# Moving table passes of a setup to the scalar engine, and starting a fold between two tables

## The chip, the core and the metric

The kernel runs on one core of a Trainium2 chip. The profile shows five engines: TensorE (PE; its weight loads are PEld), VectorE (DVE), ScalarE (ACT), GpSimd (POOL) and the sync engine (SP). They run side by side (in the first 24 us of the kernel before, TensorE, VectorE, ScalarE and GpSimd are busy for 10.5, 20.4, 20.6 and 18.7 us), and it shows what each waits for. Here GpSimd starts the loads. The metric is the device time of one execution in microseconds (us). The kernel before is steady: 49 runs of it in this study lie between 609.36 and 610.03 us, mean 609.66.

## The reference

```python
X = np.fft.fft(np.fft.fft(x, axis=1), axis=2).real     # x: 8 x 3008 x 256
h = np.maximum(X.transpose(0, 2, 1) @ w_tok1, 0) @ w_tok2
u = X + h.transpose(0, 2, 1)
out = u + np.maximum(u @ w_ch1, 0) @ w_ch2
```

The Fourier transforms are done as matrix products, so the kernel first makes tables of cosines and sines on the chip. This setup, the first 24 us of 608, is all that the change touches.

## The kernel before

The setup has four strands that meet in the first real product `pw`:

- the angles `vp`, `vq`, reduced to one period on VectorE and ScalarE, and their sines `tp`, `tq` on ScalarE;
- two turned copies `tt` of each table: TensorE transposes, ScalarE evicts (copies the finished accumulator away, so that it is free again), TensorE multiplies by an anti-identity (`pr`, a matrix with ones on the other diagonal), ScalarE evicts again;
- the cosine table of the first product, `td0` and `td1`, out of the angles `md`;
- batch 0: rows `xp` and, by two gathers (loads by an index list), `xm` are loaded, the fold adds and subtracts mirrored halves on VectorE (12 pieces, giving `eo`), `front` multiplies them (`pz`) and evicts to `z`.

```python
def reduced(v, r, m, period):                 # on VectorE; TWO23 is 2**23, added to round
    ts(v, m, 1.0 / period, AT.mult, TWO23, AT.add)
    ts(v, v, -TWO23, AT.add, -float(period), AT.mult)
    nc.vector.tensor_tensor(out=r, in0=v, in1=m, op=AT.add)

def filler(n):                                # products whose result nobody reads
    pw = ps_out("filler")
    for _ in range(n):
        nc.tensor.matmul(pw[:, 0:P], lhsT=ident[:], rhs=ident[:], start=True, stop=True)

# front(b): six blocks of five products, three accumulators in rotation
for t0 in (11, 6, 1):
    for half in range(2):
        pz = ps_f("pz")
        for k in range(5):
            nc.tensor.matmul(pz[:, 96*k:96*k+96], lhsT=eo[:, t0+k, c], rhs=..., ...)
        copy(b == 0 and half and t0 < 11, zo[...], pz[...])   # true: VectorE, false: ScalarE
        yield
# two small pz blocks (yield after each), then the pw products ...

# ... cut: index columns, loads, identity tables, angles ...
ts(md[:, 0:128], jrow[:, 1:129], pcol[:], AT.mult, 64.0, AT.add)
ts(md[:, 128:255], jrow[:, 1:128], pcol[:], AT.mult)
reduced(vd[:], md[:], md[:], 256)
# ... cut ...
table_d()                                     # the two sines td, then small corrections on GpSimd
turn(tp, tts_p, 8)                            # transposes, then 8 fillers
turn_rows(tts_p, 1.0, 0)
take(fold(0, [nc.vector] * 4), 12)
own = front(0)
take(own, 2)
turn(tq, tts_q, 4)
take(own, 4)
turn_rows(tts_q, -1.0, 0)
take(own, 2)
filler(8)
take(own, 2)                                  # the first pw products
```

Of the kernel before, what the change touches and what calls it, by code (L numbers as in the profile page):

```python
# [9 lines left out]
FP16 = mybir.dt.float16  # L10
FP32 = mybir.dt.float32
I32 = mybir.dt.int32
AT = mybir.AluOpType
AFT = mybir.ActivationFunctionType
# [5 lines left out]
P = 128  # L20
BB = 8
S = 3008
D = 256
DTOK = 256
# [5 lines left out]
NG = 12  # L30
# [5 lines left out]
TWO23 = float(2.0 ** 23)  # L36
# [4 lines left out]
def kernel(  # L41
# [9 lines left out]
    nc = tc.nc  # L51
# [8 lines left out]
    const = ctx.enter_context(tc.tile_pool(name="const", bufs=1))  # L60
# [5 lines left out]
    def ps_mm(name):  # L66
        return psum.tile([P, 512], FP32, tag="mm", name=name, bufs=3)
# [7 lines left out]
    def dram(t, offset, ap):  # L75
        return bass.AP(tensor=t, offset=offset, ap=ap)

    def iota(t, pattern, base, cm):
        nc.gpsimd.iota(t, pattern=pattern, base=base, channel_multiplier=cm,
                       allow_small_or_imprecise_dtypes=True)  # L80

    def pvec(name, dt=FP32):
        return const.tile([P, 1], dt, tag=name, name=name)

    def ts(out_, in_, s1, op0, s2=None, op1=None, eng=nc.vector):
        if op1 is None:
            eng.tensor_scalar(out=out_, in0=in_, scalar1=s1, scalar2=None, op0=op0)
        else:
            eng.tensor_scalar(out=out_, in0=in_, scalar1=s1, scalar2=s2,
                              op0=op0, op1=op1)  # L90



    pcol, xicol, qcol = (pvec(n) for n in ("pcol", "xicol", "qcol"))
    iota(pcol[:], [[0, 1]], 0, 1)
    ts(xicol[:], pcol[:], float(NQ), AT.is_ge)
    nc.vector.scalar_tensor_tensor(out=qcol[:], in0=xicol[:], scalar=-float(NQ),
                                   in1=pcol[:], op0=AT.mult, op1=AT.add)
# [5 lines left out]
    jrow = const.tile([P, 129], FP32, tag="jrow")  # L104
# [3 lines left out]
                                   op0=AT.mult, op1=AT.add)  # L108
    ts(rowi[:], rowi[:], -2.0, AT.mult)
    ts(ix8[:], ix8f[:], rowi[:], AT.add, 0.0, AT.max)  # L110

    x8 = dram(x_t, 0, [[8 * D, BB * S // 8], [1, 8 * D]])

# [20 lines left out]
    def gdma(out_, in_):  # L134
        nc.gpsimd.dma_start(out=out_, in_=in_)


    setup = ctx.enter_context(ExitStack())
    stage = setup.enter_context(tc.tile_pool(name="stage", bufs=1))
    gen = setup.enter_context(tc.tile_pool(name="gen", bufs=1))  # L140
    w1p = stage.tile([P, NG, DTOK], FP16, tag="w1p")
    w1m = stage.tile([P, NG, DTOK], FP16, tag="w1m")
    tp, tq = (const.tile([P, NG, P], FP16, tag=n, name=n) for n in ("tp", "tq"))
    nc.scalar.activation(out=pvec("sin0")[:], in_=pcol[:], func=AFT.Sin, scale=0.0)
    for t in (tp, tq):
        for i in range(2):
            h = slice(64 * i, 64 * i + 64)
            nc.scalar.activation(
                out=t[h, :, 64 - 64 * i:128 - 64 * i],
                in_=pcol[h, :].unsqueeze(2).to_broadcast([64, NG, 64]),  # L150
                func=AFT.Copy, scale=0.0)
    nc.scalar.activation(out=w1m[64:128, NG - 1, :],
                         in_=pcol[64:128, :].to_broadcast([64, DTOK]),
                         func=AFT.Copy, scale=0.0)

    x_tiles = {0: load_x(0)}

# [7 lines left out]
                                   op0=AT.mult, op1=AT.add)  # L165
# [6 lines left out]
                                   op0=AT.mult, op1=AT.add)  # L172
    nc.vector.scalar_tensor_tensor(out=reff[:], in0=eq32[:], scalar=1472.0, in1=reff[:],
                                   op0=AT.mult, op1=AT.add)
# [3 lines left out]
                                   op0=AT.mult, op1=AT.add)  # L178
    nc.vector.scalar_tensor_tensor(out=offq[:], in0=mid[:], scalar=-752.0, in1=tmp[:],
                                   op0=AT.mult, op1=AT.add)  # L180
# [40 lines left out]
    def reduced(v, r, m, period):  # L221
# [4 lines that stand above are left out]
    def sin(out_, in_, period):  # L226
        nc.scalar.activation(out=out_, in_=in_, func=AFT.Sin, scale=PI2 / period)

    def table3(tab, r):
        for i in range(2):  # L230
            h = slice(64 * i, 64 * i + 64)
            sin(tab[h, :, h], r[h, :, :], S)
# [12 lines left out]
            copy(0, tts[0][:, 768 * h:768 * h + 768], pt[:, 0:768])  # L245
        filler(warm)

    def turn_rows(tts, sgn, warm):
        for h in range(3):
            pr = ps_mm("pr")  # L250
            nc.tensor.matmul(pr[:], lhsT=anti[:], rhs=tts[0][:, 512 * h:512 * h + 512],
                             start=True, stop=True)
            nc.scalar.activation(out=tts[1][:, 512 * h:512 * h + 512], in_=pr[:],
                                 func=AFT.Copy, scale=sgn)
        filler(warm)


    def filler(n):
        pw = ps_out("filler")
        for _ in range(n):  # L260
            nc.tensor.matmul(pw[:, 0:P], lhsT=ident[:], rhs=ident[:], start=True,
                             stop=True)

    def copy(e, out_, in_):
        if e:
            (nc.vector, nc.gpsimd)[e - 1].tensor_copy(out=out_, in_=in_)
        else:
# [9 lines left out]
    gp = gen.tile([P, NG], FP32, tag="gp")  # L277
    mp, vp, mq, vq = (gen.tile([P, NG, 64], FP32, tag=n, name=n)
                      for n in ("mp", "vp", "mq", "vq"))
    up, down = pvec("up"), pvec("down")  # L280
    nc.vector.memset(up[:], TWO23)
    nc.vector.memset(down[:], -TWO23)
    ts(gp[:], jrow[:, 0:NG], r2[:], AT.mult, offp[:], AT.add)
    nc.vector.scalar_tensor_tensor(
        out=mp[:], in0=jrow[:, 0:64].unsqueeze(1).to_broadcast([P, NG, 64]),
        scalar=r47[:], in1=gp[:].unsqueeze(2).to_broadcast([P, NG, 64]),
        op0=AT.mult, op1=AT.add)
# [5 lines left out]
    for o, i, scale, bias in ((mq, mp, 1.0, dq), (vq, mq, 1.0 / S, up),  # L293
                              (vq, vq, 1.0, down)):
        nc.scalar.activation(out=o[:], in_=i[:], func=AFT.Identity, scale=scale,
                             bias=bias[:])

    ident = const.tile([P, P], FP16, tag="ident")
    ts(ident[:], jrow[:, 0:P], pcol[:], AT.is_equal)
    anti = const.tile([P, P], FP16, tag="anti")  # L300
    acol = pvec("acol")
    ts(acol[:], pcol[:], -1.0, AT.mult, 127.0, AT.add)
    ts(anti[:], jrow[:, 0:P], acol[:], AT.is_equal)

    mask0, q24 = pvec("mask0"), pvec("q24")
    ts(mask0[:], xicol[:], -1.0, AT.mult, 1.0, AT.add)
    ts(q24[:], qcol[:], 24.0, AT.add)
# [3 lines left out]
    for a, n, col, off in ((0, 2, qcol, 47 / 4), (2, 2, qcol, 0.0), (4, 1, q24, 47 / 8)):  # L311
# [4 lines left out]
    sin(cs[:], m1[:], 47)  # L316
    reduced(vp[:], vp[:], mp[:], S)
    table3(tp, vp)
    nc.vector.scalar_tensor_tensor(out=vq[:], in0=vq[:], scalar=-float(S), in1=mq[:],
                                   op0=AT.mult, op1=AT.add)  # L320
    table3(tq, vq)
    for i, m in ((0, mask0), (1, xicol)):
        ts(t1n[:, :, i, :], cs[:, i:4:2, :], m[0:KR, :], AT.mult)
    ts(t1b[:, 1, :], cs[:, 4, :], float(np.sqrt(0.5)), AT.mult,
       xicol[0:KR, :], AT.mult)
    nc.vector.tensor_copy(out=t1b[:, 0:3:2, :], in_=t1n[:, :, 0, :])

    md, vd = (gen.tile([P, 255], FP32, tag=n, name=n) for n in ("md", "vd"))
    ts(md[:, 0:128], jrow[:, 1:129], pcol[:], AT.mult, 64.0, AT.add)
    ts(md[:, 128:255], jrow[:, 1:128], pcol[:], AT.mult)  # L330
    reduced(vd[:], md[:], md[:], 256)
    td0 = const.tile([P, 131], FP16, tag="td0")
    td1 = const.tile([P, P], FP16, tag="td1")
    alt = const.tile([P, 131], FP16, tag="alt")
# [3 lines left out]
    tcol, sgn = pvec("tcol"), pvec("sgn")  # L338
# [5 lines left out]
    ts(perm[:], jrow[:, 0:P], tcol[:], AT.is_equal, sgn[:], AT.mult, eng=pl)  # L344

    def table_d():
        sin(td0[:, 2:130], md[:, 0:128], 256)
        sin(td1[:, 1:P], md[:, 128:255], 256)
        pl.memset(td0[:, 0:1], 1.0)
        ts(td0[:, 1:2], td0[:, 129:130], 0.5, AT.mult, 0.5, AT.add, eng=pl)  # L350
        ts(td0[:, 130:131], td0[:, 129:130], 0.5, AT.mult, -0.5, AT.add, eng=pl)
        ts(td0[0:1, :], td0[0:1, :], 0.5, AT.mult, eng=pl)

        pl.memset(td1[:, 0:1], 0.0)
        pl.memset(td1[0:1, 0:1], 0.5)
        pl.memset(alt[:], 1.0)
        pl.memset(alt[:, 2:129:2], -1.0)
        pl.memset(alt[:, 130:131], 0.0)
# [33 lines left out]
    def fold(b, engs):  # L392
        xp, xm = x_tiles.pop(b)
        eo = perb.tile([KR, NR, D], FP16, tag="eo", name="eo")
        state[b] = {"eo": eo}
        add, sub = AT.add, AT.subtract
        for s, (t0, t1) in enumerate(((13, 17), (9, 13), (5, 9), (1, 5))):
            tt = engs[s].tensor_tensor
            t = slice(t0, t1)
            rv = slice(16 - t0, 16 - t1 if t1 < 17 else None, -1)  # L400
            if s == 0:
                tt(out=xp[:, 1:NR, 0], in0=xp[:, 1:NR, 0], in1=xm[0:KR, ::-1, 0], op=add)
                tt(out=eo[:, :, 0], in0=xp[:, :, 0], in1=xp[:, :, 0], op=add)
            tt(out=xp[:, t, 1:D], in0=xp[:, t, 1:D], in1=xm[0:KR, rv, D - 1:0:-1], op=add)
            yield
            if t0 == 1:
                t = slice(0, t1)
            tt(out=eo[:, t, 1:129], in0=xp[:, t, 1:129], in1=xp[:, t, 255:127:-1], op=add)
            yield
            tt(out=eo[:, t, 129:256], in0=xp[:, t, 1:128], in1=xp[:, t, 255:128:-1],  # L410
               op=sub)
            yield
# [304 lines left out]
    def take(g, n):  # L717
        for _ in range(n):
            next(g, None)

    table_d()
    turn(tp, tts_p, 8)
    turn_rows(tts_p, 1.0, 0)
    take(fold(0, [nc.vector] * 4), 12)
    own = front(0)
    take(own, 2)
    turn(tq, tts_q, 4)
# [31 lines left out]
    for b in range(BB):  # L759
        nxt = front(b + 1) if b + 1 < BB else iter(())  # L760
        folds = fold(b + 2, [nc.vector] * 4) if b + 2 < BB else None
        for c in range(NCH):
# [6 lines left out]
            for s in range(4):  # L769
                sub = 4 * c + s  # L770
                n = plan[b > 0][sub]
# [76 lines left out]
```

## Time and profile before

| | kernel before |
|---|---|
| time, median of the first 3 runs | 609.57 us (609.36 to 609.90) |
| first TensorE instruction | 12.36 us |
| first `pw` product | 23.32 us |
| first product into `pt`, from where TensorE works almost without a pause | 30.4 us |

Three lines of the profile's page: busy time by engine, the granted clock of TensorE in 40 slices (9 is 0.9 or more), and the engines' shares in the chain that ended last.

```profile
PE 586.7 (97%) x6278; PEld 420.1 (69%) x6278; DVE 455.8 (75%) x1021; ACT 441.2 (73%) x992; POOL 147.4 (24%) x233
...
PEclk9999999999999999999999999999999999999999
...
PE 91%; DVE 6%; ACT 2%; issue 0%; DVEq 0%; POOL 0%; POOLq 0%
```

TensorE bounds all but the setup. What the setup loses before the first `pw` shifts everything after it. The chain of waits shows who holds it up (start, duration, engine, tile, line):

```profile
9.62 0.97 DVE vp L224
...
10.61 0.84 ACT tp L227
...
14.05 0.51 ACT td L227 x2
14.56 1.40 ACT tt L268 x2
...
17.71 0.97 ACT z L268 x2
18.69 1.39 ACT tt L268 x2
20.07 0.72 ACT z L268
...
20.84 0.47 PE pz L424 x5
...
22.24 1.03 DVE z L266 x2
...
23.32 0.23 PE pw L451
```

VectorE is the chain up to 10.6 us, then ScalarE to 20.8 us. The last ScalarE `z` frees the third accumulator, and the last five `pz` products wait for it. The instructions in order of time, with the idle time before them in brackets, show room on both engines:

```profile
10.61 1.69 ACT L227 ACTIVATE tp<-vp 64x768 f16<-64x768 f32 x2 [1.71 <-DVE vp L224]
...
11.92 0.27 DVE L89 TENSOR_SCALAR md<-jrow,pcol 128x128 f32<-128x128 f32 x1
...
13.33 0.43 DVE L224 TENSOR_TENSOR md<-vd,md 128x255 f32<-128x255 f32 x1
13.68 0.21 DVE L402 TENSOR_TENSOR xp<-xp,xm 94x16 f16<-94x16 f16 x1
```

ScalarE idles 1.71 us before `tp`. VectorE spends 11.92 to 13.7 us on the angles `md`, and only then begins the fold.

### The profile page before, as it was taken

Reading aid. Unit: us, or ns where it says so; the run is one execution under the profiler, and the core shown is the slowest. Engines: PE = TensorE matmul, PEld = TensorE weight load, DVE = VectorE, ACT = ScalarE, POOL = GpSimd, SP = SyncE. Lnnn points to the kernel's source line nnn. Section 1 sums busy time; section 2 is a strip of 40 time slices with the busy share of each in tenths; the row PEclk is TensorE's granted clock in tenths of the full one; section 3 lists DMA queues with packets and bytes.
Section 4 is the critical chain, followed back from the end, with each engine's and each line's share of the span. In section 5 each row is a group of like instructions: output and inputs, shape, how many; then the busy total and the mean of one; then the engine's idle time right before and its main releaser. Section 6 shows DMA issues by size and latency. Waiting matters only on the chain.

```text
span 607.9 us, 15617 instructions
## 1 busy us (share of the span) xinstructions
PE 586.7 (97%) x6278; PEld 420.1 (69%) x6278; DVE 455.8 (75%) x1021; ACT 441.2 (73%) x992; POOL 147.4 (24%) x233
## 2 busy tenths in 40 slices
PE   1999999999999999999999999999999999999996
PEld 1756767667777677766777667766687667766675
DVE  8869689658887598757988689756979666665672
ACT  8876886777777777686777777677776877767772
POOL 8400414111242112401314222411131112111131
PEclk9999999999999999999999999999999999999999
DMA  9994924733249535673429233493341423234524
GB/s 150 210 190 104 179 57 82 134 69 78 54 91 158 70 53 86 107 117 53 91 51 176 62 76 75 77 178 53 53 74 47 92 54 83 58 70 60 90 58 100
DMA packets 86601, 56.53 MB, mean 93 GB/s; under 512 B 54864, under 2 KB 83472, under 8 KB 85776
## 3 DMA queue, kind: packets, MB, share of 16 engines
q1 hardware_dynamic: 78048, 37.84, 34.0%
q0 software_dynamic: 8256, 17.49, 16.6%
q8 instruction: 49, 0.80, 0.5%
q14 instruction: 24, 0.20, 0.1%
q10 hardware_dynamic: 224, 0.20, 0.1%
HBM read 34.98 MB, written 24.64 MB: 98 GB/s over the span
## 4 chain that ended last, share of the span: by engine, by line
PE 91%; DVE 6%; ACT 2%; issue 0%; DVEq 0%; POOL 0%; POOLq 0%
PE pc L583 39%; PE px L624 23%; PE py L624 9%; PE pu L543 7%; PE po L681 4%; PE pt L473 3%; PE pz L424 2%; DVE w L454 1%; PE py L501 1%; PE pq L501 1%; PE pw L451 1%; PE pw L452 1%; DVE sb L600 1%; ACT tt L268 0%; DVE osb L609 0%
## 5 line engine op out<-in xcount | busy, mean ns | idle before, releaser
L586 ACT ACTIVATE c<-pc 128x512 f16<-128x512 f32 (+1 forms) x572 | 295.9, 595 | 38.8 <-PE pc L583 20.8
L609 POOL TENSOR_TENSOR osb<-osb,rt 128x256 f32<-128x256 f32 x84 | 81.2, 967 | 377.5 <-DVE osb L609 367.7
L583 PE MATMUL pc<-ut,wc1p 128*128 128x512 f16 x576 | 140.5, 379 | 0.0
L624 PEld LDWEIGHTS <-c 128*128 128x128 f16 x2016 | 121.4, 98 | 20.7 <-issue 1.3
L583 PE MATMUL pc<-ut,wc1m 128*128 128x512 f16 (+1 forms) x576 | 134.9, 370 | 0.0
L551 DVE TENSOR_TENSOR ut<-pu,yt 128x512 f16<-128x512 f32 (+1 forms) x96 | 64.6, 674 | 53.3 <-PE pu L543 53.1
L624 PEld LDWEIGHTS <-sb 128*128 128x128 f16 x1512 | 89.9, 98 | 10.8 <-DVE sb L600 0.7
L629 ACT ACTIVATE m<-px 128x256 f32<-128x256 f32 x126 | 48.5, 385 | 66.9 <-PE px L624 41.5
L583 PEld LDWEIGHTS <-wc1p 128*128 128x128 f16 x576 | 52.1, 98 | 49.2 <-issue 2.6
L583 PEld LDWEIGHTS <-wc1m 128*128 128x128 f16 x576 | 53.0, 98 | 46.4
L624 PE MATMUL px<-wst,c 128*128 128x128 f16 x1008 | 70.8, 219 | 0.2 <-DVE c L600 0.2
L624 PE MATMUL px<-wc,c 128*128 128x128 f16 x1008 | 63.1, 219 | 0.0
L268 ACT ACTIVATE z<-pz 128x480 f16<-128x480 f32 (+1 forms) x60 | 40.2, 673 | 16.9 <-PE pz L424 11.0
L600 DVE TENSOR_TENSOR sb<-sb,c 128x768 f16<-128x768 f16 x84 | 50.2, 598 | 2.9
L609 DVE TENSOR_TENSOR osb<-py,m 128x256 f32<-128x256 f32 x84 | 35.1, 418 | 22.2 <-ACT m L629 17.4
L600 DVE TENSOR_TENSOR sb<-c 128x768 f16<-128x768 f16 x84 | 49.3, 587 | 2.4 <-ACT c L586 2.4
L543 PE MATMUL pu<-w2p,uu 128*128 128x512 f16 (+1 forms) x168 | 50.0, 379 | 0.0
L454 DVE SCALAR_TENSOR_TENSOR w<-alt,pw 128x131 f16<-128x131 f16 x96 | 33.0, 350 | 21.1 <-ACT w L268 20.5
L600 DVE TENSOR_TENSOR sb<-c,sb 128x768 f16<-128x768 f16 x84 | 47.1, 561 | 0.0
L600 DVE TENSOR_TENSOR c<-c 128x768 f16<-128x768 f16 x84 | 46.5, 554 | 0.0
L508 DVE TENSOR_TENSOR yt<-py,qs 128x512 f16<-128x512 f32 x48 | 30.9, 685 | 15.2 <-ACT qs L504 15.0
L624 PE MATMUL py<-wst,sb 128*128 128x128 f16 x504 | 35.2, 219 | 0.5 <-DVE sb L600 0.5
(163 smaller groups left out, 678.4 us busy)
## 6 DMA issues: line engine op xcount, KB each, us to landing
out_dram<-osb SPq DMA_DIRECT2D x83, 256.0 KB, 3.7
xp<-in_x_dram POOLq DMA_DIRECT2D x16, 272.0 KB
out_dram<-osb SPq DMA_DIRECT2D x11, 192.0 KB, 3.2
xp<-in_x_dram POOLq DMA_DIRECT2D x16, 127.5 KB
rt<-ut SPq DMA_TRANSPOSE x96, 3.8
w2s<-in_moe_w_tok_dram POOLq DMA_DIRECT2D x1, 1504.0 KB
w1p<-in_moe_w_tok_dram POOLq DMA_DIRECT2D x2, 384.0 KB
wc<-in_moe_w_ch_dram POOLq DMA_DIRECT2D x1, 768.0 KB
```

What stands on the lines that cost most here:

```text
L268: nc.scalar.activation(out=out_, in_=in_, func=AFT.Copy)
L454: nc.vector.scalar_tensor_tensor(out=w[:, g, 0:131], in0=alt[:], scalar=pw[:, 131:132], in1=pw[:, 0:131], op0=AT.mult, op1=AT.add)
L508: nc.vector.tensor_tensor(out=yt[:, h, CW * c:CW * c + CW], in0=py[:], in1=qs[:], op=op)
L543: nc.tensor.matmul(pu[:, 0:n], lhsT=uu[:, th, int(minus), h, :], rhs=w2_cols(b, c)[:, th], start=(th == 0), stop=(th == 1))
L551: nc.vector.tensor_tensor(out=ut[:, h, 0:n].rearrange("p (a b) -> p a b", b=64), in0=pu[:, 0:n].rearrange("p (b a) -> p a b", b=64), in1=y ...
L583: nc.tensor.matmul(pc[:, 0:n], lhsT=wc[:, h, ct * P:(ct + 1) * P], rhs=ut[:, h, 0:n], start=(h == 0), stop=(h == 1))
L586: nc.scalar.activation(out=c1[:, ct, 0:n], in_=pc[:, 0:n], func=AFT.Relu)
L600: nc.vector.tensor_tensor(out=o, in0=x, in1=y, op=op)
L609: eng.tensor_tensor(out=o, in0=x, in1=y, op=AT.add)
L624: nc.tensor.matmul(o[:, t], lhsT=a(k)[:, f:f + P], rhs=w(k), start=(first and t == 0 and k == 0), stop=(k == HC - 1), skip_group_check=True)
L629: nc.scalar.activation(out=m[:, i], in_=pa[:, 0], func=AFT.Copy)
L681: nc.tensor.matmul(po[0:n, o:o + D], lhsT=c1[:, ct, ks * P:ks * P + n], rhs=wc2[:, ct, :], start=(ct == 0), stop=(ct == NCT - 1))
```

## The change

Its intent is to give ScalarE's idle time work that VectorE does, and to start the fold earlier. The passes over `md` and `vd` go to ScalarE, ahead of its zero fills, which stay on it. The identity tables come after `vp` on VectorE. The last pass over `md` and the two `td` sines come after six of the twelve fold pieces. The argument `on_vector` of `turn_rows`, which the change also adds, is never used.

```diff
+    nc.scalar.activation(out=md[:, 0:128], in_=jrow[:, 1:129], func=AFT.Identity,
+                         scale=pcol[:], bias=quarter[:])
+    nc.scalar.activation(out=md[:, 128:255], in_=jrow[:, 1:128], func=AFT.Copy,
+                         scale=pcol[:])
+    for i, scale, bias in ((md, 1.0 / 256, up), (vd, 1.0, down)):
+        nc.scalar.activation(out=vd[:], in_=i[:], func=AFT.Identity, scale=scale,
+                             bias=bias[:])
     # ... the zero fills of tp, tq, w1m, moved up with these ...
-    ident / anti built before the angle reductions
     reduced(vp[:], vp[:], mp[:], S)
     table3(tp, vp)
+    ident / anti built here; the pass over vq after the t1n tables
-    ts(md[:, 0:128], jrow[:, 1:129], pcol[:], AT.mult, 64.0, AT.add)
-    ts(md[:, 128:255], jrow[:, 1:128], pcol[:], AT.mult)
-    reduced(vd[:], md[:], md[:], 256)
     def table_d():
+        nc.vector.scalar_tensor_tensor(out=md[:], in0=vd[:], scalar=-256.0, in1=md[:],
+                                       op0=AT.mult, op1=AT.add)
         sin(td0[:, 2:130], md[:, 0:128], 256)
-    table_d()
     turn(tp, tts_p, 8)
     turn_rows(tts_p, 1.0, 0)
-    take(fold(0, [nc.vector] * 4), 12)
+    pieces = fold(0, [nc.vector] * 4)
+    take(pieces, 6)
+    table_d()
+    take(pieces, 6)
```

(The two lines on the identity tables stand for moved blocks. The constants `up`, `down` and `quarter` are filled earlier too, which is cut here.)

More of the change, by code (lines that the diff above doesn't have):

```diff
@@ L90, in ts @@
                               op0=op0, op1=op1)
+    setup = ctx.enter_context(ExitStack())
+    stage = setup.enter_context(tc.tile_pool(name="stage", bufs=1))
+    gen = setup.enter_context(tc.tile_pool(name="gen", bufs=1))
+    w1p = stage.tile([P, NG, DTOK], FP16, tag="w1p")
+    w1m = stage.tile([P, NG, DTOK], FP16, tag="w1m")
+    tp, tq = (const.tile([P, NG, P], FP16, tag=n, name=n) for n in ("tp", "tq"))
+    up, down, quarter = (pvec(n) for n in ("up", "down", "quarter"))
+    nc.vector.memset(up[:], TWO23)
+    nc.vector.memset(down[:], -TWO23)
+    nc.vector.memset(quarter[:], 64.0)
     pcol, xicol, qcol = (pvec(n) for n in ("pcol", "xicol", "qcol"))
@@ L110 @@
     ts(ix8[:], ix8f[:], rowi[:], AT.add, 0.0, AT.max)
+    nc.scalar.activation(out=pvec("sin0")[:], in_=pcol[:], func=AFT.Sin, scale=0.0)
+    md, vd = (gen.tile([P, 255], FP32, tag=n, name=n) for n in ("md", "vd"))
+    nc.scalar.activation(out=md[:, 0:128], in_=jrow[:, 1:129], func=AFT.Identity,
[5 more added lines that the diff above has]
+                             bias=bias[:])
+    for t in (tp, tq):
+        for i in range(2):
+            h = slice(64 * i, 64 * i + 64)
+            nc.scalar.activation(
+                out=t[h, :, 64 - 64 * i:128 - 64 * i],
+                in_=pcol[h, :].unsqueeze(2).to_broadcast([64, NG, 64]),
+                func=AFT.Copy, scale=0.0)
+    nc.scalar.activation(out=w1m[64:128, NG - 1, :],
+                         in_=pcol[64:128, :].to_broadcast([64, DTOK]),
+                         func=AFT.Copy, scale=0.0)
     x8 = dram(x_t, 0, [[8 * D, BB * S // 8], [1, 8 * D]])
@@ L135, in gdma @@
         nc.gpsimd.dma_start(out=out_, in_=in_)
-    setup = ctx.enter_context(ExitStack())
-    stage = setup.enter_context(tc.tile_pool(name="stage", bufs=1))
-    gen = setup.enter_context(tc.tile_pool(name="gen", bufs=1))
-    w1p = stage.tile([P, NG, DTOK], FP16, tag="w1p")
-    w1m = stage.tile([P, NG, DTOK], FP16, tag="w1m")
-    tp, tq = (const.tile([P, NG, P], FP16, tag=n, name=n) for n in ("tp", "tq"))
-    nc.scalar.activation(out=pvec("sin0")[:], in_=pcol[:], func=AFT.Sin, scale=0.0)
-    for t in (tp, tq):
-        for i in range(2):
-            h = slice(64 * i, 64 * i + 64)
-            nc.scalar.activation(
-                out=t[h, :, 64 - 64 * i:128 - 64 * i],
-                in_=pcol[h, :].unsqueeze(2).to_broadcast([64, NG, 64]),
-                func=AFT.Copy, scale=0.0)
-    nc.scalar.activation(out=w1m[64:128, NG - 1, :],
-                         in_=pcol[64:128, :].to_broadcast([64, DTOK]),
-                         func=AFT.Copy, scale=0.0)
     x_tiles = {0: load_x(0)}
@@ L246, in turn, with turn_rows @@
         filler(warm)
-    def turn_rows(tts, sgn, warm):
+    def turn_rows(tts, sgn, warm, on_vector=()):
         for h in range(3):
@@ L252, in turn_rows @@
                              start=True, stop=True)
-            nc.scalar.activation(out=tts[1][:, 512 * h:512 * h + 512], in_=pr[:],
-                                 func=AFT.Copy, scale=sgn)
+            o = tts[1][:, 512 * h:512 * h + 512]
+            if h in on_vector:
+                ts(o, pr[:], sgn, AT.mult)
+            else:
+                nc.scalar.activation(out=o, in_=pr[:], func=AFT.Copy, scale=sgn)
         filler(warm)
@@ L279 @@
                       for n in ("mp", "vp", "mq", "vq"))
-    up, down = pvec("up"), pvec("down")
-    nc.vector.memset(up[:], TWO23)
-    nc.vector.memset(down[:], -TWO23)
     ts(gp[:], jrow[:, 0:NG], r2[:], AT.mult, offp[:], AT.add)
@@ L296 @@
                              bias=bias[:])
-    ident = const.tile([P, P], FP16, tag="ident")
-    ts(ident[:], jrow[:, 0:P], pcol[:], AT.is_equal)
-    anti = const.tile([P, P], FP16, tag="anti")
-    acol = pvec("acol")
-    ts(acol[:], pcol[:], -1.0, AT.mult, 127.0, AT.add)
-    ts(anti[:], jrow[:, 0:P], acol[:], AT.is_equal)
     mask0, q24 = pvec("mask0"), pvec("q24")
@@ L318 @@
     table3(tp, vp)
-    nc.vector.scalar_tensor_tensor(out=vq[:], in0=vq[:], scalar=-float(S), in1=mq[:],
-                                   op0=AT.mult, op1=AT.add)
-    table3(tq, vq)
+    ident = const.tile([P, P], FP16, tag="ident")
+    ts(ident[:], jrow[:, 0:P], pcol[:], AT.is_equal)
+    anti = const.tile([P, P], FP16, tag="anti")
+    acol = pvec("acol")
+    ts(acol[:], pcol[:], -1.0, AT.mult, 127.0, AT.add)
+    ts(anti[:], jrow[:, 0:P], acol[:], AT.is_equal)
     for i, m in ((0, mask0), (1, xicol)):
@@ L326 @@
     nc.vector.tensor_copy(out=t1b[:, 0:3:2, :], in_=t1n[:, :, 0, :])
-    md, vd = (gen.tile([P, 255], FP32, tag=n, name=n) for n in ("md", "vd"))
-    ts(md[:, 0:128], jrow[:, 1:129], pcol[:], AT.mult, 64.0, AT.add)
-    ts(md[:, 128:255], jrow[:, 1:128], pcol[:], AT.mult)
-    reduced(vd[:], md[:], md[:], 256)
+    nc.vector.scalar_tensor_tensor(out=vq[:], in0=vq[:], scalar=-float(S), in1=mq[:],
+                                   op0=AT.mult, op1=AT.add)
+    table3(tq, vq)
     td0 = const.tile([P, 131], FP16, tag="td0")
@@ L346, in table_d @@
     def table_d():
+        nc.vector.scalar_tensor_tensor(out=md[:], in0=vd[:], scalar=-256.0, in1=md[:],
+                                       op0=AT.mult, op1=AT.add)
         sin(td0[:, 2:130], md[:, 0:128], 256)
```

## The prediction

> **What bounds the kernel now.** The page shows TensorE busy 97% of the 607.9 us span at 0.9 or more of its clock in every slice; the chain that ended last is 91% PE. Only the first stretch is not PE's: it begins at 12.36 us and is fed properly only from about 23.3 us. Busy time by stretches gives for 0 to 24 us: PE 10.5, DVE 20.4, ACT 20.6. The change touches only this stretch (the instruction order is otherwise the same), so the stake is a shift of everything after 24 us, a few us at most.
>
> **The chain of waits** is DVE up to 10.6 us (identity tables 0.58 us, `vp` ready at 10.58). From 10.61 to 20.79 it is almost wholly ACT, without a gap: sines of `tp`, `tq` (3.4 us), two `td` sines (0.5), `tt` copies (1.4), `tt` from `pr` (1.8), `z` (1.1), `tt` (1.4), `z`. ACT sat idle 1.71 us before `tp`, for DVE `vp`.
>
> **What the change moves.**
> 1. DVE loses five passes over `md`/`vd` (11.92 to 13.7 us in the timeline, about 1.75 us) and gains one combined pass (this form took 0.95 at 768 elements; estimate for 255: 0.4), after six fold pieces.
> 2. ACT gains four passes. 768 elements with one pointer operand took 0.94[...]. Zero fills, `mq`, `vq`, `cs` move later by this; `cs` ends at 10.2 to 10.6 instead of 8.9.
> 3. The identity tables leave the path to `vp`: ready near 9.95 instead of 10.58.
>
> ACT's idle 1.71 us is thus eaten by its new passes: `tp` begins at 10.1 to 10.55 instead of 10.61. `tq` waits for DVE `vq`, now after the identities and `t1n`: 12.0 to 12.2 (was 12.33).
>
> 4. The fold could begin on DVE near 12.1 instead of 13.68, but its data are not there: the landing times in the trace put the end of the second `xm` gather at 13.0 us. The fold starts near 13.05 after almost 1 us of idle, six pieces end near 16.5 (17.1 before), the `md` pass near 16.9.
> 5. The `td` sines leave the place before `tt` but stand before the first `z`; ACT must still do both before `z`. `tt` starts 0.6 to 0.8 us earlier, `z` only 0.1 to 0.3 us (17.3 to 17.5, was 17.60).
>
> From there ACT's order is unchanged. So of about 1.35 us net taken from DVE only 0.1 to 0.3 us reaches the first `pw` product (23.32 before), and the rest shifts with it. GpSimd's next load issues move 1.5 to 2 us later, but into a busy DMA queue.
>
> **Predicted time:** 609.35 us, range 608.8 to 609.8. Chances: faster by over 2% 0.01, within 2% 0.98, slower by over 2% 0.01.
>
> **What would show it.** ACT's idle before `tp` falls from 1.7 to under 0.5; the first DVE fold instruction at 12.9 to 13.2, with about 1 us idle before it ended by a DMA; the first `z` on ACT at 17.2 to 17.6; the first `pw` at 23.0 to 23.3.
>
> **What would make it wrong.** ACT's passes longer than estimated, so that `tp` starts after 10.6; the GpSimd corrections of `td` or `alt` delaying the first `w`; a different landing time; another phase of the PE-bound part, worth tenths.

The four terms for ScalarE's new passes, less overlaps, came to 1.3 to 1.75 us, and this is what "move later by this" stands for; the times given for `cs`, `tp` and what follows rest on this sum.

## The result

The changed kernel took 610.62 us (median of 6 runs, 609.52 to 611.18). The kernel before took 609.59 us in 6 runs (609.36 to 609.96). The ratio is 1.0013, with a 95% interval of 1.0000 to 1.0025. Ratios here are the mean time of one kernel's runs over that of the other's of the same rounds, so not quite the ratio of the medians.

The six times were 609.52, 610.74, 610.70, 610.53, 611.18 and 609.76: two like the kernel before, four a microsecond longer. The profiled run was the fastest of them. Its chain of waits:

```profile
10.66 0.73 ACT tp L240
...
13.99 1.52 ACT tt L284 x2
...
17.28 0.51 ACT td L240 x2
17.79 0.96 ACT z L284 x2
18.75 1.38 ACT tt L284 x2
20.14 0.72 ACT z L284
...
20.90 0.37 PE pz L433 x5
...
22.21 1.03 DVE z L282 x2
...
23.29 0.23 PE pw L460
```

The moves happened as intended. ScalarE now runs from 0.73 us without a gap before `tp` (whose first sine starts at 10.57 us; it was 10.61), and `tt` joins the chain 0.57 us earlier (13.99, was 14.56; it starts 0.47 us earlier). But the `td` sines now stand between `tt` and `z`, and the first `z` is at 17.79 (was 17.71). The first `pw` is at 23.29, as before. In the order of time:

```profile
2.13 0.48 ACT L125 ACTIVATE md<-jrow,quarter,pcol 128x128 f32<-128x128 f32 x1
2.52 0.38 ACT L127 ACTIVATE md<-jrow,pcol 128x127 f32<-128x127 f32 x1
2.94 0.51 ACT L130 ACTIVATE vd<-md,up 128x255 f32<-128x255 f32 x1
...
10.57 1.68 ACT L240 ACTIVATE tp<-vp 64x768 f16<-64x768 f32 x2
...
12.25 0.23 DVE L411 TENSOR_TENSOR xp<-xp,xm 94x16 f16<-94x16 f16 x1
...
19.91 0.81 DVE L282 CAST z<-pz 128x480 f16<-128x480 f32 x1 [0.87 <-PE pz L433]
21.30 0.66 DVE L282 CAST z<-pz 128x480 f16<-128x480 f32 x1 [0.58 <-PE pz L433]
```

The fold begins 1.43 us earlier than in the profiled run of the kernel before, and much of the time so won turns up as idle time of VectorE before its `z` evictions, 0.87 and 0.58 us (0.29 and 0.17 before). That is the fast run: nothing won. It does not say where the slow ones lose a microsecond. On TensorE one thing is new. The last `pz` products of the changed kernel, and two groups of fillers:

```profile
18.44 0.63 PE L277 MATMUL filler<-ident 128*128 128x128 f16 x4
18.87 1.41 PE L433 MATMUL pz<-t1n,eo 94*128 94x96 f16 x15
20.90 0.37 PE L433 MATMUL pz<-t1n,eo 94*128 94x96 f16 x5 [0.62 <-ACT z L284]
...
22.36 0.62 PE L277 MATMUL filler<-ident 128*128 128x128 f16 x8
```

TensorE does the earlier products sooner and then idles 0.62 us for the same accumulator. And four fillers take 0.63 us at 18.4 us where eight take 0.62 us at 22.4: TensorE works at about half its later speed in the first place (the fillers start 0.107 us apart there, 0.057 us at 22.4). The trace of the kernel before has the same, eight fillers each time:

```profile
13.62 1.06 PE L261 MATMUL filler<-ident 128*128 128x128 f16 x8
...
22.39 0.61 PE L261 MATMUL filler<-ident 128*128 128x128 f16 x8
```

### The profile page after: what moved, and what is told of

Same layout as the page of the kernel before. It is cut to its first block, busy times and chain, and to the rows that moved or that the text cites. A ratio compares the mean times of both kernels' runs of the same rounds, so it can differ in the third digit from the quotient of the medians.

```text
span 607.7 us, 15619 instructions
## 1 busy us (share of the span) xinstructions
PE 586.5 (97%) x6278; PEld 420.0 (69%) x6278; DVE 453.8 (75%) x1018; ACT 442.7 (73%) x996; POOL 150.1 (25%) x233
## 4 chain that ended last, share of the span: by engine, by line
PE 91%; DVE 4%; ACT 4%; issue 1%; DVEq 0%
PE pc L592 39%; PE px L633 23%; PE py L633 9%; PE pu L552 7%; PE po L690 4%; PE pt L482 3%; PE pz L433 2%; DVE w L463 1%; PE py L510 1%; PE pq L510 1%; PE pw L460 1%; PE pw L461 1%; DVE sb L609 1%; ACT tt L284 0%; DVE osb L618 0%
## 5 line engine op out<-in xcount | busy, mean ns | idle before, releaser
L595 ACT ACTIVATE c<-pc 128x512 f16<-128x512 f32 (+1 forms) x572 | 295.8, 594 | 38.8 <-PE pc L592 20.7
L618 POOL TENSOR_TENSOR osb<-osb,rt 128x256 f32<-128x256 f32 x84 | 83.0, 988 | 377.6 <-DVE osb L618 364.6
L633 PEld LDWEIGHTS <-c 128*128 128x128 f16 x2016 | 121.4, 98 | 20.7 <-issue 1.3
L609 DVE TENSOR_TENSOR sb<-c 128x768 f16<-128x768 f16 x84 | 51.2, 609 | 2.3 <-ACT c L595 2.3
```

What stands on the lines that cost most here:

```text
L595: nc.scalar.activation(out=c1[:, ct, 0:n], in_=pc[:, 0:n], func=AFT.Relu)
L609: nc.vector.tensor_tensor(out=o, in0=x, in1=y, op=op)
L618: eng.tensor_tensor(out=o, in0=x, in1=y, op=AT.add)
L633: nc.tensor.matmul(o[:, t], lhsT=a(k)[:, f:f + P], rhs=w(k), start=(first and t == 0 and k == 0), stop=(k == HC - 1), skip_group_check=True)
```

## A theory, and its rivals

The clock records (the times in a trace at which the granted clock changes) of the two first traces show full clock from 21.06 us in the kernel before and from 20.63 us in the changed one, each time for 587.09 us. The fillers before these times stand at the slower pace and those after them at the faster. (The page's clock line and the windows view show 1.00 also before the first record, as from 13.81 to 17.22 us of the changed kernel, where the fillers start 0.107 us apart. So early durations must be read from the instructions.) What sets the clock the records do not say. My guess was that it follows how much work TensorE had just before.

- **Theory A.** In the changed kernel TensorE has too little to do somewhere between 17 and 24 us. In some runs the clock is then at one half (as first put, because it steps up late) while the `pw` and `ph` products, which are the first that TensorE itself bounds, are waiting.
- **Theory B.** The changed schedule is a microsecond slower or more variable in itself, by its transfers or its engines, and the clock only goes along.
- **Theory C.** It is the added ScalarE passes or the later loads that cost, not the split of the fold.

Fourteen batches of five or six runs were made to tell these apart. The columns and the landing times below were counted from the records of the traces. Where one says "window", read 3.41 us, the length of each of the three dips of the clock told of below (23.68 to 27.09, 22.47 to 25.88 and 12.25 to 15.66 us).

## The experiments

### Both kernels again, with more and with fewer fillers

The kernel before unchanged:

> The kernel before, unchanged, to list the granted clock of each of its runs. Theory A ([...]the changed kernel leaves TensorE idle too much between 17 and 24 us[...]): all runs 609.3 to 610.0 us, mean clock 1.0 (0.9995 or more) in each. Theory B (the changed schedule itself, its DMA or its engines, is about 1 us slower or more variable, the clock only an accompaniment): same times, and clocks scattered as in the changed kernel (0.997 to 1.0).

Measured: 609.59 to 609.85 us, median 609.68. The mean clocks were 0.998 to 1.0, which looked like theory B. The two first traces suggest why: full clock ends 587.09 us after it began, in the changed kernel at 607.72 us of a span of 607.75, when TensorE has no work left (0.00 us busy from 604.3 us on). By my estimate it ends earlier where it begins earlier (a mean of 0.998 would be 2.4 us at one half). So the mean clock does not tell the groups apart as expected; that part of the expectation was wrong. It does tell one thing: a dip to one half as long as the one in the slow trace below (3.41 us) takes 0.0028 off the mean (half of 3.41 us in 609), so a run at 0.998 or above had none once its full clock had begun.

The changed kernel unchanged:

> The changed kernel, unchanged. Theory A: two groups of runs, 609.4 to 609.8 and 610.5 to 611.3 us, and the slow ones have the lower clock (0.997 to 0.999); median about 610.5. Theory B: one spread around 610.5, times and clocks not tied to each other.

Measured: 609.64, 610.02, 610.50, 609.60, 609.78 us. One slow run only, so the median (609.78) was not where it was expected.

The changed kernel with more fillers:

```diff
     turn(tq, tts_q, 4)
-    take(own, 4)
+    take(own, 3)
+    filler(5)
+    take(own, 1)
     turn_rows(tts_q, -1.0, 0)
     take(own, 2)
-    filler(8)
+    filler(11)
```

> The changed kernel with eight more filler matmuls in the two places where TensorE idled (5 before the last five-matmul block of pz, 3 more before the first pw). Theory A: the slow group goes, all runs within 609.3 to 610.0, clock 1.0. Theory B: no change against the changed kernel, median 610.3 to 610.8.

Measured: 609.53 to 609.74 us, median 609.61. As theory A says, but with one slow run of five in the control this alone would prove little; it is repeated below.

The kernel before with fewer fillers:

```diff
-    turn(tq, tts_q, 4)
+    turn(tq, tts_q, 0)
     ...
-    filler(8)
+    filler(0)
```

> The kernel before without its 4 filler matmuls after the transposes of tq and its 8 before the first pw. Theory A: it now shows the slow group too: some runs 610.5 to 611.5 with a clock of 0.997 to 0.999, median above 610. Theory B: unchanged, 609.3 to 610.0 (fillers carry no data).

Measured: 611.33, 611.16, 609.70, 609.75, 611.35 us. Twelve products whose result nobody reads are taken away and three of five runs lose 1.5 us. The profiled run was slow: its records show full clock from 20.26 to 23.68 us, half to 27.09, full again, and its mean clock is 0.995. So in this run the clock does not come late, as theory A first had it. It comes, and falls back for 3.41 us.

### A slow run of the changed kernel

> The changed kernel once more, for a trace of a slow run and for its share. Theory A, refined with the traces so far: [...]about 45% of the runs should be at 610.4 to 611.3 and the rest at 609.5 to 610.0; a trace of a slow run shows half the clock for one window after about 22 to 24.3 us. Rival B: the slow runs have full clock there and lose the time elsewhere (a transfer landing late, for example).

Measured: 610.76, 609.47, 609.57, 610.61, 610.60 us; three of five slow, where the expectation had about 45%, and the profiled run was the slowest. Its windows view, cut at the clock's changes and in steps of 3.41 us (busy time by engine, then the granted clock, the share of the DMA engines and GB/s):

```profile
15.64:19.06 3.42, 2.82 (x43) 2.18 (x42) 3.35 (x8) 3.40 (x8) 2.31 (x6) 1.00 1.47 198
19.06:22.47 3.41, 1.75 (x19) 1.19 (x19) 1.80 (x4) 3.16 (x7) 3.27 (x9) 1.00 1.16 226
22.47:25.88 3.41, 3.28 (x24) 2.47 (x22) 1.61 (x5) 1.74 (x5) 0.40 (x1) 0.50 1.04 215
25.88:29.30 3.42, 3.42 (x38) 3.15 (x37) 3.26 (x10) 2.97 (x10) 1.00 (x1) 1.00 1.04 206
```

In the stretch to 22.47 us TensorE was busy 1.75 of 3.41 us; in the next one its clock is 0.50, and VectorE and ScalarE, who wait for its products, fall to about half their work (1.61 and 1.74 us busy, then 3.26 and 2.97). The same in the instructions of TensorE:

```profile
20.72 0.37 PE L433 MATMUL pz<-t1n,eo 94*128 94x96 f16 x5 [1.71 <-ACT z L284]
...
23.11 0.29 PE L460 MATMUL pw<-td,z 128*128 128x128 f16 x1
...
23.94 0.42 PE L380 MATMUL ph<-w1p,tt 128*128 128x256 f16 x1
24.16 0.42 PE L382 MATMUL ph<-w1m,tt 128*128 128x256 f16 x1
...
26.11 0.27 PE L382 MATMUL ph<-w1m,tt 128*128 128x256 f16 x1
26.21 0.27 PE L380 MATMUL ph<-w1p,tt 128*128 128x256 f16 x1
```

A `ph` product starts every 0.21 us at 24 us and every 0.11 us at 26 us. In this run the full clock came early, at 15.64 us (the ten `pz` products at 16.01 us take 0.59 us; in the first trace, at 16.36, they take 1.00). That made TensorE fast where it was not needed: it ran ahead, idled 1.71 us for ScalarE's `z`, and so left little work in the 3.41 us before the dip from 22.47 to 25.88 us. The first `pw` is even early (23.11), but the first product into `pt` stands at 31.51 us instead of 30.39. Over all sixteen traces the time of the run lies 579.1 to 579.5 us after this product, so the 1.1 us by which the dip delays it are nearly all of the slow run's loss (610.76 against 609.52). The second gather of `xm` had landed at 12.20 us, no later than in fast runs, so the late transfer of rival B is not there.

How much work did TensorE have just before? I counted the columns that the products begun in a stretch of 3.41 us stream (128 for a transpose or filler, 96 for a `pz`, 512 for a `pr`; the small `pz` have 24 or 72). The stretches of three traces before their clock records, counted back from the record in steps of 3.41 us (the clock in the first four is read from the pace of the products):

| stretch | clock in it | columns | TensorE busy, us | clock in the next |
|---|---|---|---|---|
| before, 14.24 to 17.65 | half | 2,880 | 2.67 | half |
| before, 17.65 to 21.06 | half | 3,744 | 3.30 | full |
| changed, 13.81 to 17.22 | half | 3,264 | 3.06 | half |
| changed, 17.22 to 20.63 | half | 3,360 | 3.05 | full |
| `e2_after`, 19.06 to 22.47 | full | 3,000 | 1.75 | half |

In these five the stretches with 2,880, 3,000 and 3,264 columns come before half clock and those with 3,360 and 3,744 before full, while busy times of 3.06 and 3.05 us stand on the two sides. Five counts fit theory A; that the columns set the clock, and where an edge would lie, they do not show. Sixteen runs of the changed kernel in three batches gave 8 below 610.1, mean 609.67, and 8 at 610.5 to 611.2, mean 610.70.

The mean clocks split the eight slow runs. The three slowest (610.74, 610.76 and 611.18 us) have 0.997, and one of them is the trace above. The other five (610.50 to 610.70 us) have 0.999 or 1.0, too high for a dip of 3.41 us after full clock had begun. That in these the first step to full clock came late is my estimate, from how near the counts lie (3,360 before the step in the first trace, 3,264 where there was none; 3,744 before the step in the kernel before). No trace shows such a run, so for these five the late step is argued and not shown.

### The passes without the split

```diff
+    table_d()
     turn(tp, tts_p, 8)
     turn_rows(tts_p, 1.0, 0)
-    pieces = fold(0, [nc.vector] * 4)
-    take(pieces, 6)
-    table_d()
-    take(pieces, 6)
+    take(fold(0, [nc.vector] * 4), 12)
```

> The change without its split of the fold: the table passes stay on ScalarE, but the cosine sines stand before the transposes and the fold is whole, as in the kernel before. Theory A: TensorE's work up to 24 us stands where it stood before (pr at 15.2 to 15.4, the last pz block with less than 0.4 us of idle before it), so no slow group: all runs 609.3 to 610.0, median 609.5. Rival C (the added ScalarE passes or the later loads are what costs): still runs above 610.4.

Measured: 609.42 to 609.90 us, median 609.67, ratio 1.0000. No slow run. The passes on ScalarE, the late identity tables and the later loads cost nothing, and win nothing: first `pw` at 23.38 us. Theory C falls, as far as five runs can tell (if half of the runs were slow, five fast ones would be chance once in 32), and the slow runs need the split.

### Full clock from the start

A filler that runs from 2.1 us on, and more fillers in between, were to take the clock out of play:

```diff
+    wz = const.tile([P, P], FP16, tag="wz")
+    nc.vector.memset(wz[:], 0.5)
     ...
+    pz0 = ps_out("prewarm")
+    for _ in range(110):
+        nc.tensor.matmul(pz0[:, 0:P], lhsT=wz[:], rhs=wz[:], start=True, stop=True)
-    turn(tp, tts_p, 8)
-    turn_rows(tts_p, 1.0, 0)
+    turn(tp, tts_p, 20)
+    turn_rows(tts_p, 1.0, 6)
     ...
-    turn(tq, tts_q, 4)
-    take(own, 4)
+    turn(tq, tts_q, 10)
+    take(own, 3)
+    filler(8)
+    take(own, 1)
     ...
-    filler(8)
+    filler(14)
```

> The changed kernel with 110 filler matmuls on a constant tile from 2.1 us on, and more fillers between its products[...]. Theory A: [...]no slow group[...], so 608.6 to 609.3, median 608.9, in a band of 0.4 us. Theory B: as the changed kernel, median 609.8 to 610.6.

> The kernel before with the same fillers. Theory A: 608.7 to 609.4, and within 0.2 us of the changed kernel with the same fillers (the change itself is worth 0 to 0.2 us once the clock is out of play). Theory B: as the kernel before, 609.5 to 610.0, and 0.8 us or more faster than the changed kernel with the same fillers.

Measured: changed kernel 609.50, 610.34, 610.70, 610.05, 609.54 us; kernel before 609.59 to 609.83. Theory A's expectations both missed, and the medians (610.05 and 609.67) lie where theory B put them, though 0.38 us apart and not 0.8. In the trace of the changed kernel TensorE has full clock from 7.50 us to the end (the twelve transposes at 12.30 us take 0.84 us, and 1.46 in the first trace), and the first `pw` is at 23.09 us, 0.2 us earlier and no more: up to 20.65 us the chain of this trace is ScalarE's. And the slow runs did not go. The slowest (610.70) has a mean clock of 0.999. If its full clock began as early as in the trace, that is too high for a dip, and in this version something else costs too. In the kernel before, the clock fell back at 12.25 us, where TensorE idled 2.40 us for the table (its twelve transposes at 12.47 us take 1.46 us), and came back at 15.66 us. Its median of 609.67 us shows no harm from that.

The slow runs of this version were tried once more, with 16 more fillers between 18 and 20.7 us:

```diff
-    take(own, 3)
-    filler(8)
+    take(own, 2)
+    filler(10)
+    take(own, 1)
+    filler(14)
```

> The changed kernel with the early fillers, whose slow runs (3 of 5 above 610.0) had no trace, and 16 more fillers between 18 and 20.7 us. [...]the slow runs go: all within 609.4 to 610.0. If the slow runs have another cause they stay.

(The condition was that TensorE still had too little work there for the clock to stay full.)

Measured: 610.10, 609.34, 610.21, 609.93, 610.16 us. The profiled run took 610.10 and has full clock from 15.27 us on (the transposes at 17.66 us take 0.84 us), so here it is something else:

```profile
17.11 0.71 PE L435 MATMUL pz<-t1n,eo 94*128 94x96 f16 x10 [0.47 <-DVE eo L419]
...
17.75 0.51 ACT L242 ACTIVATE td<-md 128x128 f16<-128x128 f32 x2 [0.26 <-DVE md L356]
```

TensorE waits for the fold and ScalarE for `md`, which comes after six fold pieces. The fold began at 14.00 us in this run, because the second gather of `xm` landed at 13.88; the chain of waits begins with that gather. It also holds 0.78 us of the added fillers, which stand before the last `pz` block. In the three traces with early fillers it landed at 12.79, 13.88 and 13.97 us, in the thirteen others at 12.00 to 13.12. Why it landed late, and whether the early fillers caused it, is open; the slow runs of `e2_after_prewarm` have no trace. This way of taking the clock out of play failed, so theory B is not excluded for the versions with early fillers.

### The fillers once more, and the accumulator that the chain waits for

> The changed kernel with eight more fillers, a second time. Theory A: again no run above 610.0 (the changed kernel without them had 8 of 16 runs above 610.4, so ten of ten below would be chance once in a thousand); median 609.4 to 609.7. Theory B: two or three of five runs above 610.4.

Measured: 609.19 to 609.78 us, median 609.64. With the first time, ten of ten runs are below 609.8, where 8 of 16 runs without the eight fillers are above 610.4. The eight fillers carry no data and take the slow runs away, as theory A says, so I hold the clock to be the cause of the slow runs, whether it falls back or steps up late. The fillers bring no gain over the kernel before (ratio 0.9999).

So the other question remains: where is the VectorE time that the change frees? If ScalarE's `z` at 20 us holds the chain, VectorE, which idles 0.87 us there, should take it:

```diff
-            copy(b == 0 and half and t0 < 11, zo[...], pz[...])
+            copy(b == 0 and (t0 == 6 or half and t0 == 1), zo[...], pz[...])
     ...
-    filler(8)
+    filler(12)
```

> The changed kernel with the first z of the second group evicted by VectorE, which idles 0.87 us there, instead of by ScalarE, and four more fillers before the first pw. If the chain before the first pw runs over ScalarE (its z at 20.0 us frees the accumulator of the last pz block), the last pz block comes 0.4 to 0.6 us earlier, the first pw at 22.7 to 22.9 instead of 23.29, and fast runs are at 609.0 to 609.3. If something else bounds it, the first pw stays at 23.2 or later and the time at 609.5. By theory A the slow group should be gone or nearly[...].

Measured: 608.77, 608.42, 609.59, 608.48, 608.77 us, ratio 0.9987 (0.9974 to 1.0000). The chain of waits of the profiled run:

```profile
5.28 7.21 DMA xm<-in_x_dram,ix
12.61 0.24 DVE xp L411
...
18.83 0.49 DVE eo L419
19.32 0.72 DVE z L282
20.08 0.37 PE pz L433 x5
...
21.40 1.03 DVE z L282 x2
...
22.48 0.23 PE pw L460
```

The first `pw` comes 0.81 us earlier than in the changed kernel's first trace, more than expected, and four of the five runs are below the expected 609.0. (The one at 609.59 has no trace.) ScalarE is off the chain: it now runs from the gather's landing over the whole fold on VectorE.

A further step moved three `pr` products behind the small `pz` blocks:

```diff
-    take(own, 4)
+    take(own, 6)
     turn_rows(tts_q, -1.0, 0)
-    take(own, 2)
     filler(12)
```

> The same, and the three products pr of the second table are put behind the last small pz products instead of before them. Expected if TensorE's order holds the small pz back[...]: first pw another 0.3 us earlier, 22.4 to 22.6, and 608.7 to 609.1. If VectorE's evictions bound it (its z passes are then back to back), no further gain.

Measured: 609.15, 609.29, 611.23, 608.88, 608.95, 608.89 us. A miss of the expected gain: the first `pw` of the profiled run is at 22.70 us, 0.22 us later than without the swap. With the swap the gather landed 0.36 us later (12.85, was 12.49), which covers the difference, so neither a gain nor a loss by the swap itself is shown. The one run at 611.23 us has a mean clock of 0.997, which leaves room for a dip of 3.41 us (0.0028); that run has no trace, so a dip is not shown.

Last, the same eviction in the kernel before, and the version with the change again:

> The kernel before with the same move of one z to VectorE and the same four fillers. If the gain of 0.8 us seen with the changed kernel needs the VectorE time that the change frees, little is gained here: the fold ends near 20 us, so VectorE cannot take that z earlier than ScalarE did; first pw at 23.1 to 23.4, 609.4 to 609.9. If the move alone makes the gain, first pw near 22.5 and 608.5 to 608.9.

Measured: 609.27 to 609.66 us, median 609.49, ratio 0.9998. In the order of time:

```profile
19.46 0.48 DVE L410 TENSOR_TENSOR eo<-xp 94x635 f16<-94x635 f16 x1
19.96 1.99 DVE L266 CAST z<-pz 128x480 f16<-128x480 f32 x3
```

VectorE comes out of the fold at 19.96 us and cannot take the `z` earlier than ScalarE did; first `pw` at 23.21. The move alone brings nothing clear of the noise (its mean is 0.13 us below the kernel before in the same batch). It needs the time that the change frees.

> The changed kernel with the move, a second time (four of five runs were at 608.4 to 608.8, one at 609.6). If the chain now begins with the landing of the gather, first pw stands 9.9 us after that landing and the time 579.2 us after the first product into pt: 608.4 to 609.3, none above 610.

Measured: 608.84, 608.57, 609.13, 608.96, 609.55 us, ratio 0.9990 (0.9977 to 1.0004). Both times together: ten runs, 608.42 to 609.59, mean 608.91, which is 0.75 us below the mean of the kernel before and 0.76 below that of the changed kernel's fast runs (0.79 and 0.62 us against the kernel before in the same batches). No run above 610, but one above the expected 609.3. The intervals of the single batches reach 1.0, but eight of the ten runs are faster than every one of the 49 runs of the kernel before, and the first `pw` (22.48 and 22.20 us) says why. This is the fastest version. Its profiled run had the gather at 12.00 us and the first `pw` 10.2 us after it, not 9.9 as expected. The fold began 0.12 us after the landing as before; 0.17 us went into its second pass, which took 0.40 us (0.23 in `e3_zdve`). Why is open.

## Why the prediction was wrong

- **"And the rest shifts with it"** is the step that failed. The prediction let 0.1 to 0.3 us reach the first `pw` product and everything after it move rigidly. It took the clock as given, with TensorE "at 0.9 or more of its clock in every slice". The page's line does show 9 from the first slice on, but fillers at 13.6 us took 0.13 us each and those at 22.4 us 0.08, which stood in the trace before the prediction. In the slow trace the rest did not shift rigidly: TensorE was early with its products, was busy for only 1.75 of the 3.41 us up to 22.47, and then had a clock of 0.50 for 3.41 us while it was needed, and the first product into `pt` came 1.1 us late. Half of the runs (8 of 16) are about 1.0 us slower. For the clock as their cause speak ten of ten runs with fillers, and twelve fillers taken from the kernel before. That in five of the eight slow runs it stepped up late instead is argued only.
- **"Another phase of the PE-bound part, worth tenths"** was the nearest the prediction came to it, with the wrong place (in the slow trace the loss is at 23 to 27 us, not in the long part) and the wrong size (1.1 us).
- **The gain of 0.1 to 0.3 us** was not there: 8 fast runs of the changed kernel have a mean of 609.67 us, 49 runs of the kernel before 609.66. The mechanism was right, the terms were too kind. The four passes moved ScalarE's later work by 1.76 us, the top of the estimate (1.3 to 1.75): `cs` ended at 10.67 us (10.2 to 10.6 said), `tp` started at 10.57 us (10.1 to 10.55 said), `tt` at 13.99 instead of 14.46, 0.47 us earlier (0.6 to 0.8 said), the first `z` at 17.70 (17.3 to 17.5 said, 17.60 before).
- **ScalarE's idle time eaten by its new passes** was right: 1.71 us became none, and the passes took 0.48, 0.38, 0.51 and 0.51 us.
- **The fold held by the gather** was right in kind: in every trace with the split it starts 0.12 or 0.13 us after the landing. The landing was taken from one trace (13.0 us) as if it were fixed; it was 12.13 in the first trace after, so VectorE did not idle before the fold. It did not matter, as ScalarE held the chain.
- **`td` must still be done before `z`**, and ScalarE's order holds the chain up to the `z` at 20 us: right, and shown by `e3_zdve`.

## What to carry to other kernels

Here work taken from an engine off the chain won nothing until a piece of the chain was handed to it: the freed VectorE time was worth 0.75 us only after one eviction moved to it, and that eviction alone brought nothing clear of the noise (0.13 us). Where a schedule reaches TensorE's busy part through a thin stretch, as here, look at what a change leaves TensorE to do there: in the slow trace work brought forward left 1.71 us of idle time behind it, and the clock fell to 0.50. Eight fillers there took the slow runs away (ten of ten below 609.8 us). And when a profile falls on a fast run, look at the list of all times first: two groups of runs need a trace of each.
